# Second batch's Q, K and tail transposes: DMA transposes by halves of the heads in place of identity matmuls

## The chip, the cores and the metric

One core of one Trainium2 chip. The metric is device microseconds (us) of one execution, taken as the median of several. Most executions of one kernel agree within 0.3%; a run over 1.5% above the fastest of the same kernel is called slow, and only fast runs are compared. Positions are times from the start of the profiled execution's span, which is about 1.5 to 2 us shorter than the time of the run.

## The reference, cut to what matters

Cosine attention on 8 batches of 12 heads of 448 x 64, then a Fourier mix, a layer norm and a two-layer feed-forward (FFN):

```python
q_n = q / (norm(q) + 1e-6); k_n = k / (norm(k) + 1e-6)
attn = softmax(q_n @ k_n.T / tau)            # 448 x 448 per head
x    = (attn @ v) as (batch, 448, 768)
u    = x + real(fft(fft(x, axis=1), axis=2))
out  = u + relu(layernorm(u) @ w_ch1) @ w_ch2   # 768 -> 3072 -> 768
```

## The kernel before

Attention of batch b+1 runs beside the FFN of batch b, so that TensorE always has FFN matmuls to put between the attention's. A program-wide list scheduler fixes each engine's order when the kernel is built. Every change of a dependency can therefore reorder instructions far from it.

A batch's 12 heads are handled as six pairs. In the first two batches Q and K come in by halves of three pairs. Of the 448 rows, 384 are "main" and 64 are "tails". For each half: squares on ScalarE (ACT), sums and reciprocal norms, then scaling on VectorE (DVE) into bf16 buffers, then a transpose, because the scores need the head's 64 features on partitions.

The buffers that scaling writes in the second batch:

```python
qh = [[qf[:, 1152 * g:1152 * g + 1152], qf[:, 2304:3456], qf[:, 3456:3840]] for g in range(2)]   # K, Q, tails
```

The transposes, by multiplying with an identity, one pair at a time (j = 0, 1, 2), each with its eviction from PSUM:

```python
for j in range(3):
    def fn(pe, ...):                                    # K of pair j
        for t in range(3):
            r = pe.matmul(PS[.., 128*t:128*t+128], kh[:, 384*j+128*t : ..+128], ID, start=True, stop=True)
    P.add("pe", fn, ...);  evac(tile, self.KT[:, jj, :], 384, ...)
    def fn(pe, ...):                                    # Q of pair j: rows interleaved by 3, tail, column 448
        o3 = o[:, 0:384].rearrange("p (k t) -> p t k", t=3)
        for t in range(3): pe.matmul(o3[:, t], q3[:, t], ID, start=True, stop=True)
        pe.matmul(o[:, 384:448], th[..], ID[:, 0:64], ...);  pe.matmul(o[:, 448:449], q3[:, 0], ID[:, 0:1], ...)
    P.add("pe", fn, ...);  evac(tile, self.QT[:, jj, 0:449], 449, ...)
self.tails(...)                                          # K tails: 3 matmuls, two copies
```

So QT of a pair is 449 columns in order. The scores read it forward and backward (NK = 225 columns each, SQ2 = 450 together):

```python
for c0, cols in ((0, slice(0, NK)), (NK, slice(S, NK - 2, -1))):
    for h in (0, 1):
        pe.matmul(PS[:, bk + h, c0:c0 + NK], KT[r, jj, kt*128:(kt+1)*128], QT[r, jj, cols], start=True, stop=True)
```

The second FFN matrix (W2) is loaded during this same stretch, in twelve chunks of 384 KB issued by GpSimd (POOL). The second batch's raw Q and K wait in memory that later holds W2, so chunks 5 to 11 are held until the scalings have read them:

```python
for c in range(5, 12):
    self.w[12 + c].deps.update(self.raw1[2] + (self.raw1[3] if c > 7 else []))
```

SyncE (SP) issues the third batch's loads of Q and K, and is also the engine that issues DMA transposes.

## Time and profile before

| | before |
|---|---|
| time, median (range) of 4 runs | 617.77 us (617.31 to 618.76) |
| span of the profiled execution, mean clock | 616.0 us, 0.994 |
| TensorE (PE) busy | 591.1 us |
| first exponential of the second batch | 76.40 us |
| last exponential of the second batch ends | 101.77 us |
| first matmul of the second batch's FFN | 129.63 us |
| from there to the end of the span | 486.4 us |

The prediction shows the busy table, the stretches and the chain of waits. The stretch table for the start of the second batch's FFN (span; busy us and count of PE, PEld, DVE, ACT, POOL; clock; DMA share; GB/s):

```profile
136.00:160.00 24.00, 24.00 (x245) 18.60 (x244) 18.64 (x46) 18.56 (x46) 0.00 (x0) 1.00 0.90 161
```

From the timeline of ACT, the end of the first half's exponentials and the beginning and end of the second half's (start, us, what):

```profile
87.17 0.55 ACT L733 ACTIVATE E<-PS 128x450 bf16<-128x450 f32 x1
...
90.91 3.33 ACT L733 ACTIVATE E<-PS 128x900 bf16<-128x900 f32 x4
...
98.72 3.05 ACT L733 ACTIVATE E<-PS 128x900 bf16<-128x900 f32 x4
```

Between the two halves ACT does 3.19 us of other work (87.72 to 90.91).

### The profile page before, as it was taken

The numbers are of one execution on the slowest core, as the hardware profiler recorded it, in microseconds if no ns is written. First come the engines' busy times: TensorE is split into PE (matmuls) and PEld (weight loads), VectorE is DVE, ScalarE is ACT, GpSimd is POOL, SyncE is SP. The second block draws the span as 40 slices with busy tenths as digits, with TensorE's granted clock in tenths as the row PEclk, the third lists the DMA queues.
The fourth block names the chain that finished last, engine by engine and source line by source line (L and its number), as shares of the span: only waits on it lengthen the run. The fifth ranks groups of instructions, "written<-read, shape, count | busy, mean of one in ns | idle before, by whom it ended". The sixth has DMA issues, their size and how long they took to land.

```text
span 616.0 us, 13590 instructions
## 1 busy us (share of the span) xinstructions
PE 591.1 (96%) x5604; PEld 384.7 (62%) x5621; DVE 389.0 (63%) x896; ACT 346.5 (56%) x690; POOL 96.3 (16%) x125
## 2 busy tenths in 40 slices
PE   4788999999999999999999999999999999999998
PEld 3567777667866666655566676566556766654464
DVE  7887987797778677877788669667643670010011
ACT  7784797247873688347745856685576125104300
POOL 8721512010004102010030130003000010010010
PEclk8899999999999999999999999999999999999999
DMA  7999998889339536973196393716720140010001
GB/s 186 120 213 217 159 181 115 95 153 183 76 72 189 122 78 94 131 168 78 30 142 132 95 173 67 162 53 104 58 40 2 53 102 1 27 39 13 1 27 77
DMA packets 187629, 62.02 MB, mean 101 GB/s; under 512 B 166704, under 2 KB 185264, under 8 KB 187568
## 3 DMA queue, kind: packets, MB, share of 16 engines
q1 hardware_dynamic: 129648, 38.35, 32.4%
q0 software_dynamic: 57920, 22.81, 28.8%
q8 instruction: 44, 0.72, 0.5%
q14 instruction: 17, 0.14, 0.1%
HBM read 51.90 MB, written 11.01 MB: 102 GB/s over the span
## 4 chain that ended last, share of the span: by engine, by line
PE 87%; DVE 6%; ACT 2%; POOL 2%; issue 2%; DMA 1%; POOLq 0%; DVEq 0%; ACTq 0%
PE PS L1000 34%; PE PS L1022 34%; PE PS L782 5%; PE PS L751 5%; PE PS L779 2%; PE PS L847 2%; PE PS L882 2%; ACT E L733 2%; DVE U L903 1%; DMA VB<-in_v_dram 1%; DVE ST L930 1%; PE PS L763 1%; PE PS L764 1%; PE PS L1097 1%; DVE OUTB L1031 0%
## 5 line engine op out<-in xcount | busy, mean ns | idle before, releaser
L1000 PE MATMUL PS<-UNT,W1b 128*128 128x256 bf16 (+3 forms) x1424 | 230.6, 315 | 3.4 <-issue 1.3
L1022 PE MATMUL PS<-W2b,hT 128*128 128x384 bf16 (+2 forms) x1343 | 229.7, 326 | 0.1
L1000 PEld LDWEIGHTS PS<-UNT,W1b 128*128 128x128 bf16 x1440 | 129.2, 98 | 87.2 <-ACT hT L1009 3.0
L1022 PEld LDWEIGHTS PS<-W2b,hT 128*128 128x128 bf16 x1344 | 128.8, 98 | 81.9 <-issue 2.6
L733 ACT ACTIVATE E<-PS 128x900 bf16<-128x900 f32 (+1 forms) x192 | 150.0, 826 | 42.6 <-PE PS L751 35.1
L1009 ACT ACTIVATE hT<-PS 128x384 bf16<-128x384 f32 (+3 forms) x170 | 81.0, 477 | 94.7 <-PE PS L1000 93.2
L1031 DVE TENSOR_TENSOR OUTB<-PS,U 128x384 f32<-128x384 f32 (+2 forms) x56 | 31.2, 557 | 116.1 <-PE PS L1022 115.2
L1052 POOL DMA_INDIRECT out_dram<-OUTB,IDX x20 | 22.0, 1099 | 328.2 <-DVE OUTB L1031 188.8
L668 DVE TENSOR_REDUCE SS<-QH 128x6 f32<-128x384 f32 x84 | 45.4, 541 | 14.0 <-ACT QH L666 13.8
L1010 DVE TENSOR_SCALAR hT<-PS 128x256 bf16<-128x256 f32 (+3 forms) x70 | 35.3, 505 | 27.6 <-PE PS L1000 26.4
L782 PE MATMUL PS<-VB,E 128*128 128x65 bf16 x1152 | 51.2, 193 | 0.0
L782 PEld LDWEIGHTS PS<-VB,E 128*128 128x128 bf16 x1152 | 47.7, 97 | 1.7
L666 ACT ACTIVATE QH<-STG 128x384 f32<-128x384 f32 x84 | 43.6, 519 | 7.2 <-DVE SS L668 4.3
L713 POOL DMA_DIRECT2D VB<-in_v_dram x24 | 25.3, 1063 | 128.7 <-PE PS L782 127.8
L751 PE MATMUL PS<-QT,KT 64*128 64x225 bf16 x576 | 43.1, 262 | 2.0 <-ACT E L733 1.7
L779 PE MATMUL PS<-VZ,E 128*128 128x130 bf16 x192 | 42.3, 220 | 1.5 <-DMA VB<-in_v_dram 1.2
L903 DVE TENSOR_TENSOR U<-SQT,X 128x384 bf16<-128x384 f32 (+3 forms) x80 | 40.8, 551 | 0.8
L675 DVE TENSOR_TENSOR QH<-STG,RN 128x768 bf16<-128x768 f32 x42 | 39.7, 950 | 0.5
L796 DVE TENSOR_TENSOR X<-PS,RD 128x512 bf16<-128x512 f32 x48 | 33.2, 691 | 1.5
L751 PEld LDWEIGHTS PS<-QT,KT 64*128 64x128 bf16 x576 | 21.3, 94 | 20.0 <-ACT E L733 8.7
L794 DVE RECIPROCAL RD<-PS 128x8 f32<-128x8 f32 x48 | 9.9, 206 | 32.2 <-PE PS L782 32.0
L857 ACT ACTIVATE Tt<-PS 128x900 bf16<-128x900 f32 (+2 forms) x15 | 13.4, 893 | 28.1 <-PE PS L847 28.1
(117 smaller groups left out, 485.4 us busy)
## 6 DMA issues: line engine op xcount, KB each, us to landing
STG<-in_q_dram SPq DMA_DIRECT2D x18, 384.0 KB, 5.0
STG<-in_k_dram SPq DMA_DIRECT2D x18, 384.0 KB, 4.0
VB<-in_v_dram POOLq DMA_DIRECT2D x24, 192.0 KB, 6.3
W1b<-in_moe_w_ch_dram POOLq DMA_DIRECT2D x12, 384.0 KB, 8.2
W2b<-in_moe_w_ch_dram POOLq DMA_DIRECT2D x12, 384.0 KB, 6.2
out_dram<-OUTB SPq DMA_DIRECT2D x7, 384.0 KB, 2.4
hT<-in_k_dram SPq DMA_DIRECT2D x2, 576.0 KB, 5.4
hT<-in_q_dram SPq DMA_DIRECT2D x2, 576.0 KB, 6.9
```

The source lines that it names most:

```text
L666: P.add("act", lambda a, sq=sq, src=buf[:, w * x:w * x + w]: a.activation(sq, src, ACTF.Square), t_act(w), pr, f"sq{i}_{b}", reads=bn, wri ...
L668: P.add("dve", lambda v, o=SS[:, i, H // ns * x:H // ns * (x + 1)], sq=sq: v.tensor_reduce(o, sq.rearrange("p (h d) -> p h d", d=DH), AX.X ...
L675: P.add("dve", lambda v, i=i, buf=buf, qh=qh: v.tensor_tensor(v3(qh), v3(buf), RN[:, i, :].unsqueeze(2).to_broadcast((128, H, DH)), AluOp. ...
L733: return a.activation(o, self.PS[:, bk:bk + nc_, 0:SQ2], ACTF.Exp, scale=1.0 / self.tau)
L751: i = pe.matmul(self.PS[:, bk + h, c0:c0 + NK], self.KT[r, jj, kt * 128:(kt + 1) * 128], self.QT[r, jj, cols], start=True, stop=True)
L779: pe.matmul(o, st(6), self.VZ[:, j, :], start=True, stop=False, skip_group_check=True)
L782: r = pe.matmul(o[:, 65 * h:65 * h + 65], st(2 * kt + h), self.VB[:, kt, 2 * j + h, :], start=False, stop=(h == 1 and kt == 2), skip_group ...
L903: return v.tensor_tensor(U[o0:o0 + n, ut, cs].rearrange("p (i e) -> p i e", e=2), src, X[i0:i0 + n, x, cs].rearrange("p (i e) -> p i e", e ...
L1000: r = pe.matmul(self.PS[:, bk, 0:n], self.W1b[:, j, ft * 128:(ft + 1) * 128], unT[:, j, cs], start=(j == 0), stop=(j == NJ - 1))
L1009: return e.activation(self.hT[:, ft, cs], self.PS[:, bk, 0:n], ACTF.Relu)
L1010: return e.tensor_relu(self.hT[:, ft, cs], self.PS[:, bk, 0:n])
L1022: r = pe.matmul(self.PS[:, bk, 0:n], self.hT[:, ft, 128 * i:128 * i + 128], self.W2b[:, ft, c0:c0 + n], start=(ft == 0), stop=(ft == NF - 1))
```

## The change

Its intent is to take 54 transposing matmuls off TensorE, and their PSUM evictions off ACT and DVE, by letting the DMA transpose K, and Q with the tails, of one half in one transfer each. The change's DMA transposes don't interleave the rows by three as the matmul's output pattern did, so Q lies in three blocks of 128 columns, and the scores read it as three interleaved thirds (a step of 128 bf16 elements between neighbours, 256 bytes), in three pieces instead of two: 225 forward, 65 of the tail, 162 backward.

```diff
+            if b == 1:
+                qt = flat(self.QT[:])[:, 1536 * g:1536 * g + 1536]
+                for nm, o, i, n, src, wr in (("K", flat(KT of the half), qh[g][0], 9, ...),
+                                             ("Q", qt, qf[:, 2304:3840], 12, ...)):
+                    self.P.add("sp", ... sy.dma_start_transpose(o, i).then_inc(sem, 16) ...)
+                ...  two tail copies (QT -> KTD), one duplicated column on POOL
+                continue
...
+            def qcols(r, jj):
+                if b != 1:
+                    return [(0, self.QT[r, jj, 0:NK]), (NK, self.QT[r, jj, S:NK - 2:-1])]
+                a, x = self.QT[r, 3 * (jj // 3), 0:1], 384 * (jj % 3)
+                return [(0, gp(a, [[1, NK // 3], [128, 3]], x)), (NK, gp(a, [[-1, 65]], 1152 + 128 * (jj % 3) + 64)),
+                        (NK + 65, gp(a, [[-1, 54], [-128, 3]], x + 383))]
...
-                        for c0, cols in ((0, slice(0, NK)), (NK, slice(S, NK - 2, -1))):
+                        for (c0, q0), (_, q1) in zip(*[qcols(r, jj) for r in rs]):
```

More of the change, by code (lines that the diff above doesn't have):

```diff
@@ L585, in first_norm @@
             self.raw1.append(sc)
+            if b == 1:
+                qt = flat(self.QT[:])[:, 1536 * g:1536 * g + 1536]
+                for nm, o, i, n, src, wr in (
+                        ("K", flat(self.KT[:, 3 * g:3 * g + 3, :]), qh[g][0], 9, qhn[g][0], [f"KT{t}" for t in range(3)]),
+                        ("Q", qt, qf[:, 2304:3840], 12, qhn[g][1] + qhn[g][2], [f"QT{t}" for t in range(4)] + ["QTd"])):
+                    o = o.rearrange("p (t c) -> p t c", c=128)
+                    self.P.add("sp", lambda sy, sem, o=o, i=i: sy.dma_start_transpose(o, i).then_inc(sem, 16), 1.45, pg[g], f"tr{nm}{g}_{b}",
+                               reads=src + [x + y for x in src for y in ("_1", "_2")], writes=[f"{x}_{3 * g + y}" for x in wr for y in range(3)],
+                               dma=(f"t{nm}{g}", 16), serve=0.3 * n)
+                tl = qt[:, 1152:1536].rearrange("p (j c) -> p j c", j=3)
+                for x in range(2):
+                    rows = slice(64 * x, 64 * x + 64)
+                    self.copy(self.KTD[rows, 3 * g:3 * g + 3, 64 * x:64 * x + 64], tl[rows, :, 64:128], 192, 4, pg[g], f"ktd{b}",
+                              reads=[f"QTd_{3 * g + y}" for y in range(3)], writes=[f"KTD{x}_{3 * g + y}" for y in range(3)])
+                self.P.add("pool", lambda p, qt=qt, tl=tl: p.tensor_copy(tl[:, :, 64:65], qt[:, 0:1152].rearrange("p (j c) -> p j c", j=3)[:, :, 0:1]), 0.2, pg[g],
+                           f"qdup{b}", reads=[f"QT0_{3 * g + y}" for y in range(3)], writes=[f"QTd_{3 * g + y}" for y in range(3)])
+                continue
             def evac(tile, dst, n, nm, wr):
@@ L747, in fn @@
                         bk, jj = self.bank(tile), ORDER[ps]
-                        for c0, cols in ((0, slice(0, NK)), (NK, slice(S, NK - 2, -1))):
-                            for h in (0, 1):
-                                r = slice(64 * h, 64 * h + 64)
-                                i = pe.matmul(self.PS[:, bk + h, c0:c0 + NK], self.KT[r, jj, kt * 128:(kt + 1) * 128],
-                                              self.QT[r, jj, cols], start=True, stop=True)
+                        rs = [slice(64 * h, 64 * h + 64) for h in (0, 1)]
+                        for (c0, q0), (_, q1) in zip(*[qcols(r, jj) for r in rs]):
+                            for h, mv in ((0, q0), (1, q1)):
+                                n = math.prod(mv.shape[1:])
+                                i = pe.matmul(self.PS[:, bk + h, c0:c0 + n], self.KT[rs[h], jj, kt * 128:(kt + 1) * 128], mv,
+                                              start=True, stop=True)
                     return i
@@ L762, in fn @@
                 bk = self.bank(tile)
-                pe.matmul(self.PS[:, bk, 0:NK], self.KTD[:, j, :], self.QT[:, j, 0:NK], start=True, stop=True)
-                return pe.matmul(self.PS[:, bk, NK:SQ2], self.KTD[:, j, :], self.QT[:, j, S:NK - 2:-1],
-                                 start=True, stop=True)
+                for c0, mv in qcols(slice(0, 128), j):
+                    n = math.prod(mv.shape[1:])
+                    r = pe.matmul(self.PS[:, bk, c0:c0 + n], self.KTD[:, j, :], mv, start=True, stop=True)
+                return r
             self.last_qk = P.add("pe", fn, 0.2, pj, f"qk{j}t_{b}", reads=qreads(j) + [f"KTD0_{j}", f"KTD1_{j}"], tiles=(tile,), acquire=tile,
```

## The prediction

> **What bounds the kernel now.** I read first the page's busy table and its 40 slices, then a table by stretches, then the chain of waits, then the order of instructions around the second batch's attention.
>
> ```profile
> PE 591.1 (96%) x5604; PEld 384.7 (62%) x5621; DVE 389.0 (63%) x896; ACT 346.5 (56%) x690; POOL 96.3 (16%) x125
> ...
> PE   4788999999999999999999999999999999999998
> DVE  7887987797778677877788669667643670010011
> ACT  7784797247873688347745856685576125104300
> ```
>
> TensorE is nearly full except in the first four slices (62 us); VectorE is high there and low at the end. The change acts once, in the second batch, so what matters is whether that batch's attention gates anything. The stretches (span, then busy us and count of PE, PEld, DVE, ACT, POOL, then clock, DMA share, GB/s):
>
> ```profile
> 68.00:92.00 24.00, 22.13 (x279) 16.73 (x278) 20.88 (x50) 20.67 (x40) 4.75 (x7) 1.00 1.13 171
> 92.00:130.00 38.00, 38.00 (x350) 26.43 (x348) 31.02 (x77) 18.18 (x39) 6.33 (x7) 1.00 0.78 111
> 130.00:136.00 6.00, 5.65 (x51) 4.21 (x49) 5.13 (x13) 3.28 (x10) 1.64 (x2) 1.00 0.91 192
> 136.00:200.00 64.00, 64.00 (x660) 46.82 (x658) 50.12 (x120) 41.76 (x92) 6.23 (x7) 1.00 0.82 129
> ```
>
> From 68 to 92 us, where Q, K and tails are transposed, TensorE idles only 24.00 - 22.13 = 1.87 us, but DVE and ACT are 86 to 87% busy. From 92 us on TensorE has no idle but 0.35 us at 130. So everything after 130 us is fixed TensorE work, and the end moves with the start of the second FFN. What sets that start, from the chain of waits (start, us, what):
>
> ```profile
> 113.22 4.89 PE PS L1022 x30
> 118.13 0.56 DVE OUTB L1031
> ...
> 123.44 0.21 DVE MV L932
> ...
> 128.93 0.06 DVE F L939
> 128.98 0.34 issue
> 129.32 0.95 DVE QH L675
> 130.27 0.48 DVE OUTB L1031
> 130.80 5.30 PE PS L1000 x45
> ```
>
> From 118 us the chain leaves TensorE and runs through VectorE: the second batch's residual, layer norm and their evictions. The timeline puts the second FFN's first matmul at 129.63 us. The two normalised tiles that it needs are ready at 126.29 us; with 2.8 us to land a transpose that is about 129.1. So TensorE runs out of first-FFN work within about half a microsecond of the second batch's tiles arriving. **Two paths are level here**: TensorE's own work, and the second batch's attention through ACT and DVE. The change shortens the first and touches the second.
>
> The order around the first half of the heads (start, us, engine, line, operation):
>
> ```profile
> 73.89 0.28 DVE L571 TENSOR_TENSOR QH<-W2b,RN 128x128 bf16<-128x128 f32 x1
> ...
> 75.36 0.56 PE L751 MATMUL PS<-QT,KT 64*128 64x225 bf16 x8
> ...
> 76.40 0.92 ACT L733 ACTIVATE E<-PS 128x900 bf16<-128x900 f32 x1
> ```
>
> Scaling of this half ends at 74.17, but by then its first pair of heads is already transposed: scores at 75.36, first exponential at 76.40. The last exponential of the batch ends at 101.77. That is 25.4 us for 24 exponentials costing 19.0 us of ACT.
>
> **What the Trainium skill says.** "DMA: Bandwidth & Descriptors", section Issuing engines are not separate DMA queues: transfers of every issuing engine share the same 16 DMA engines and interleave. The trace agrees that they are shared: a DMA share over 1 and 171 GB/s in this stretch, while weight chunks take 6.2 to 8.2 us to land. The same page, section DMA Transpose (X-bar): it works on 2-byte data and writes SBUF, so no PSUM and no eviction; the later batches use it, rows below. "TensorE: Matmul & The Clock Gate", section Part 4: PE-mode transpose: TensorE's output goes to PSUM and needs a copy after it. This kernel multiplies by an identity as an ordinary matmul, and the trace shows that copy as the evictions below. "Advanced Engine Details and Errata", section SBUF Cachelines: a read that changes the 16-byte line at each access pays a penalty. The new thirds step 128 bf16, 256 bytes. No matmul here has such a moving operand; the existing reversed one costs nothing (261 ns against 262 forward). This is open.
>
> **The change part by part.** The transposes and their evictions, from the groups by shape for 68 to 92 us (busy us, mean ns):
>
> ```profile
> L611 PE MATMUL PS<-ID,QH 128*128 128x128 bf16 x18 | 3.0, 301 | 0.1
> L590 ACT ACTIVATE QT<-PS 128x449 bf16<-128x449 f32 x4 | 2.2, 549 | 0.6 <-PE PS L613 0.3
> L590 DVE CAST KT<-PS 128x384 bf16<-128x384 f32 x4 | 2.1, 549 | 0.0
> ```
>
> *Removed from TensorE*: 54 matmuls. In the timeline a group for Q (three strided, the tail, one column) holds the array about 0.45 us, one for K 0.20, one for tails 0.16: 6 x 0.45 + 6 x 0.20 + 2 x 0.16 = 4.2 us. (Busy figures of these lines overlap their neighbours, so they aren't added.)
>
> *Added to TensorE*: each of 18 score blocks goes from 4 matmuls to 6, each of 6 tail blocks from 2 to 3: 42 more, the columns still 450. The 65-column piece can't start much faster than the warm-up matmuls of 62 columns, one per 30 ns (73 in 2.23 us). Estimate: 40 ns more a block, 24 x 0.04 = 1.0 us. Net -3.2 us if the stride is free.
>
> *Removed from ACT and DVE*: KT and QT evictions, 3.15 us on ACT and 3.37 on DVE. The tail copies stay, from SBUF now (0.3 to 0.5 us each), plus two small copies on GpSimd, 0.3 to 1.0 us each (that line in the later batches has 261 to 998 ns).
>
> *Added to the DMA*: four transposes. The present ones carry 128x768:
>
> ```profile
> QT<-QH SPq DMA_TRANSPOSE x24, 3.1
> KT<-QH SPq DMA_TRANSPOSE x18, 4.5
> ```
>
> The last number is median us from issue to landing; issuing takes 1.2 to 1.3 us, the minimum is 2.7 and the maximum 9.2. A K half is 1.5 times as large, a Q half with tails twice. By issue time alone: K 1.9 us and Q 2.5 us, and 2 us more to land; shared with weight chunks I take 6 to 8 us for Q.
>
> *Moved*: the wait becomes coarse. Q can leave only when all three pairs and tails are scaled, 74.17 less about 0.7 us of evictions no longer between: 73.5. Then 6 to 8 us of transfer, about 1.2 us for tail copy and duplicated column (in series, each with a semaphore), 0.6 us of scores and waits. The first exponential comes at 81.3 to 83.3 instead of 76.40, 5 to 7 us later. But ACT and DVE don't lose that time: they do the second half's squares, sums and scalings in it, now done at 88.44; I expect about 83, so the second half's transposes land near 90, before the first half's exponentials end (10 us after they start), and the present gap between halves, 87.72 to 90.91, closes. From the first exponential on ACT needs the 19 to 20 us of exponentials and about 2.5 us of ReLU evictions and the next batch's squares: end near 81.3 + 22.5 = 103.8 to 105.8, against 101.77. So +2 to +4 us on the attention path; less the half microsecond of slack at 129 us and about 0.7 us of lighter DVE, **+1 to +3 us** at the start of the second FFN. TensorE's 3.2 us don't show: it waits for that start.
>
> **The rivals.** (1) *The saving counts*: if transfers land in 4 us, ACT relief makes up for the late start, attention ends as before or sooner, and up to 3.2 us is gained, 615 us. For it: quiet landings of 2.7 us; against it, 171 GB/s of other traffic and the coarse wait. (2) *The SP queue blocks*: the third batch's loads leave at 83.11 us, when the weight chunk that they wait for lands, and take till 88.78 to issue. If the second half's transposes stand behind them in SP's fixed order, they land 6 to 8 us late and the end is +5 to +7, 624 us. (3) *The stride slows matmuls*: 387 of 450 columns in 24 blocks, 161 ns a block at full rate; at half rate 24 x 0.161 = 3.9 us more, which only cancels TensorE's saving, and shows as 0 to +1 us. (4) *Weight chunks come late*: 1.4 MB more, some 7 us at 200 GB/s, while the last W2 chunk lands near 102 and is used from about 106. Against it: two holes, 74 to 78 us at 103 to 127 GB/s and 82 to 84 at 45, and that the chunks gated on the scalings (three at 74.58, three at 88.86) leave earlier.
>
> **Range and chances.** The middle is 617.75 + 1.5 = 619.2 us: +1 to +3 weighted with rival 1 (about 30%) and rival 2 (about 15%). Range 614.5 to 623.5. Two per cent is 12.4 us: a gain of that size would exceed all that is removed, and a loss needs rivals 2 and 4 together. Faster 0.02, same 0.94, slower 0.04.
>
> **What would show it.** First exponential of the second batch at 81 to 83 us, no gap between its halves, last one at 104 to 106; the second FFN's first matmul 1 to 3 us after 129.63, with 3 to 5 us of TensorE idle before it where there is none now; from there to the end the same 486 us. Q transposes 6 to 8 us to landing. The 225-column score matmul at its 261 ns if the stride is free. I am wrong if the second FFN starts before 129 us, if the matmuls of the thirds are far longer, or if TensorE's idle time comes after 136 us.

## The result, and the profile after

The changed kernel took **637.62 us**, the median of all its runs (fast ones of 635.71, 637.10 and 638.14, a slow one of 648.18), against 617.77 before. Ratios in this document are the mean time of one kernel's fast runs over that of the other's fast runs of the same rounds, so not quite the ratio of the medians quoted. Here it is 1.0309, with a 95% interval of 1.028 to 1.0338: slower. The results are correct. Lines moved down by the change: the exponentials are L752 now (L733 before), the scores L778 and L792, the FFN's first product L1028 and its second L1050, the transposes L594.

The head of the page of the changed kernel (busy us and share, then tenths in 40 slices of 15.9 us):

```profile
span 635.1 us, 13600 instructions
...
PE 598.1 (94%) x5609; PEld 385.9 (61%) x5609; DVE 388.5 (61%) x889; ACT 344.5 (54%) x685; POOL 94.7 (15%) x127
...
PE   4878995987999999999999999999999999999998
...
PEclk9998997997999999999999999999999999999999
```

The span grew by 19.1 us. TensorE's busy time didn't fall but rose by 7 us. About 2 us of this rise are not real: the trace before lacks 17 matmul records (5604 matmuls beside 5621 weight loads), which leaves 2.16 us of holes from 270 to 600 us, where the trace after has none. There are two dents in its row, in the seventh slice (95 to 111 us) and in the ninth and tenth (127 to 159 us). The row of the clock falls in the seventh and the tenth too. The stretches of the changed kernel:

```profile
68.00:92.00 24.00, 22.94 (x229) 16.39 (x229) 15.92 (x40) 16.13 (x35) 6.88 (x11) 1.00 1.40 172
92.00:130.00 38.00, 30.07 (x334) 19.78 (x331) 16.69 (x42) 19.58 (x34) 5.27 (x7) 0.87 0.95 116
130.00:136.00 6.00, 6.00 (x42) 3.73 (x40) 5.63 (x12) 2.23 (x5) 1.12 (x1) 1.00 0.67 145
136.00:160.00 24.00, 17.40 (x131) 12.40 (x130) 18.66 (x45) 10.80 (x35) 1.20 (x2) 0.86 0.68 130
```

From 92 to 130 us TensorE lost 7.93 us and from 136 to 160 us 6.60 us, where before there was no hole in either stretch. DVE did 16.69 us of work from 92 to 130 us where it did 31.02 before: the second batch's work hadn't arrived. What held it is in the chain of waits (start, us, what):

```profile
84.53 1.95 PE PS L1050 x12
87.05 2.55 ACT E L752 x3
89.83 14.44 DMA QT<-QH
104.27 0.74 issue
105.01 0.64 PE PS L778 x6
...
141.53 0.93 DVE ST L958 x2
146.79 21.86 PE PS L1028 x180
```

One transfer, the Q transpose of the second half, carries 14.44 us of the chain. TensorE's own rows in the timeline name the same two waits (the bracket holds the idle time just before, and what ended it):

```profile
105.01 1.07 PE L778 MATMUL PS<-QT,KT 64*128 64x225 bf16 x12 [5.74 <-DMA QT<-QH]
...
146.79 0.80 PE L1028 MATMUL PS<-UNT,W1b 128*128 128x256 bf16 x3 [6.60 <-DVE SS L687]
```

The releaser in the second row is only the one that came last by the profile; the weight load just before that matmul waited for "DMA UNT<-F", the transposes of the normalised tiles, which began at 141.56 us. That is the second batch arriving late at its FFN.

What became of the four transposes. SP's timeline (start, issue time, what; each transfer ends some time after its issue):

```profile
72.20 1.35 SPq L594 DMA_TRANSPOSE KT<-QH  x1
75.14 3.71 SPq L594 DMA_TRANSPOSE QT<-QH  x1
82.42 2.03 SPq L594 DMA_TRANSPOSE KT<-QH  x1
88.41 0.62 SPq L679 DMA_DIRECT2D STG<-in_q_dram  x1
89.08 0.65 SPq L679 DMA_DIRECT2D STG<-in_k_dram  x1
89.83 10.36 SPq L594 DMA_TRANSPOSE QT<-QH  x1
```

From issue to landing these took 7.4, 9.5, 6.9 and 14.4 us. Between the third and the fourth stand two loads of the third batch, and SP's table of waits shows how long they held the queue (us in total, times, longest):

```profile
SPq L679 <- DMA W2b<-in_moe_w_ch_dram: 3.9, 1, 3.9
```

The two loads of 192 KB each landed after 10.1 and 12.1 us, at 98.47 and 101.2. From 89.83 to 98.47 us, the first 8.6 us of Q's flight, SP's queue moved 0.39 MB, which is just what the two loads hold, and in every trace here SP's transfers land in the order of their issue. So Q's transpose stood behind the loads in flight too, and not only for the 2.5 us before its issue.

And the exponentials, from ACT's timeline:

```profile
87.05 3.04 ACT L752 ACTIVATE E<-PS 128x900 bf16<-128x900 f32 x4 [2.10 <-PE PS L778]
...
97.47 0.55 ACT L752 ACTIVATE E<-PS 128x450 bf16<-128x450 f32 x1 [0.57 <-PE PS L792]
104.29 0.36 ACT L1089 ACTIVATE KTD<-QT 64x192 bf16<-64x192 bf16 x1 [6.28 <-DMA QT<-QH]
105.67 3.00 ACT L752 ACTIVATE E<-PS 128x900 bf16<-128x900 f32 x4 [0.61 <-PE PS L778]
...
118.77 0.55 ACT L752 ACTIVATE E<-PS 128x450 bf16<-128x450 f32 x1 [0.18 <-PE PS L792]
```

Together with the rows before, these give the whole account of the second batch's attention:

| stretch | before | changed | difference |
|---|---|---|---|
| first exponential starts | 76.40 | 87.05 | +10.65 |
| from it to the end of the first half's exponentials | 11.32 | 10.97 | -0.35 |
| gap between the halves | 3.19 | 7.65 | +4.46 |
| second half's exponentials | 10.86 | 13.65 | +2.79 |
| last exponential ends | 101.77 | 119.32 | **+17.55** |
| second FFN's first matmul | 129.63 | 146.79 | **+17.16** |
| from there to the end | 486.4 | 488.3 | +1.9 |

While the second half's exponentials run, TensorE feeds them at half clock: the granted clock was 0.50 from 104 to 112 us, and again 0.50 from 144 to 148, late in the holes of 5.74 and 6.60 us and after them. The clock is not the whole of the 2.79 us, as e1 below shows. Its mean was back at 0.91 in 112 to 116 us and at 1.00 from 116 us. The kernel before shows 1.00 in all these stretches.

Groups of score matmuls by shape, 80 to 125 us of the changed kernel (count | busy us, mean ns | idle before). The means hold some at half clock:

```profile
L778 PE MATMUL PS<-QT,KT 64*128 64x225 bf16 x36 | 7.2, 394 | 7.8 <-DMA QT<-QH 5.7 <-ACT E L752 1.9
L778 PE MATMUL PS<-QT,KT 64*128 64x162 bf16 x36 | 6.0, 326 | 0.0
L778 PE MATMUL PS<-QT,KT 64*128 64x65 bf16 x36 | 3.8, 204 | 0.0
```

So there are four suspects: the landing time of the transposes beside other traffic (A), the place of Q's second transpose behind two loads (B), the strided read of Q (C), and the coarse hand-over by halves itself (D).

### The profile page after: what moved, and what is told of

The parts are those of the page before. It is cut to its first block, busy times and chain, and to the rows that moved or that the text cites. A ratio compares the mean times of both kernels' runs of the same rounds, so it can differ in the third digit from the quotient of the medians.

```text
span 635.1 us, 13600 instructions
## 1 busy us (share of the span) xinstructions
PE 598.1 (94%) x5609; PEld 385.9 (61%) x5609; DVE 388.5 (61%) x889; ACT 344.5 (54%) x685; POOL 94.7 (15%) x127
## 4 chain that ended last, share of the span: by engine, by line
PE 87%; DVE 4%; DMA 3%; POOL 2%; issue 2%; ACT 2%; POOLq 0%; DVEq 0%; ACTq 0%
PE PS L1028 35%; PE PS L1050 34%; PE PS L778 5%; PE PS L810 5%; DMA QT<-QH 2%; PE PS L875 2%; PE PS L807 2%; PE PS L910 2%; ACT E L752 2%; PE PS L792 1%; DMA VZ<-in_v_dram 1%; DVE U L931 1%; PE PS L1125 1%; DVE ST L958 1%; POOL VB L732 1%
## 5 line engine op out<-in xcount | busy, mean ns | idle before, releaser
L1028 PE MATMUL PS<-UNT,W1b 128*128 128x256 bf16 (+3 forms) x1440 | 233.0, 317 | 7.9 <-DVE SS L687 6.6
L1050 PE MATMUL PS<-W2b,hT 128*128 128x384 bf16 (+2 forms) x1344 | 230.6, 327 | 0.0
L1028 PEld LDWEIGHTS PS<-UNT,W1b 128*128 128x128 bf16 x1440 | 129.8, 98 | 94.0 <-DMA UNT<-F 7.0
L1050 PEld LDWEIGHTS PS<-W2b,hT 128*128 128x128 bf16 x1344 | 128.7, 98 | 82.9 <-issue 3.8
L752 ACT ACTIVATE E<-PS 128x900 bf16<-128x900 f32 (+1 forms) x192 | 149.7, 824 | 51.4 <-PE PS L778 44.0
L1080 POOL DMA_INDIRECT out_dram<-OUTB,IDX x20 | 20.6, 1031 | 316.8 <-DVE OUTB L1059 251.2
L778 PE MATMUL PS<-QT,KT 64*128 64x225 bf16 (+2 forms) x612 | 46.8, 269 | 10.5 <-DMA QT<-QH 5.7
L778 PEld LDWEIGHTS PS<-QT,KT 64*128 64x128 bf16 x612 | 23.2, 96 | 31.2 <-ACT E L752 11.8
```

What stands on the lines that cost most here:

```text
L752: return a.activation(o, self.PS[:, bk:bk + nc_, 0:SQ2], ACTF.Exp, scale=1.0 / self.tau)
L778: i = pe.matmul(self.PS[:, bk + h, c0:c0 + n], self.KT[rs[h], jj, kt * 128:(kt + 1) * 128], mv, start=True, stop=True)
L1028: r = pe.matmul(self.PS[:, bk, 0:n], self.W1b[:, j, ft * 128:(ft + 1) * 128], unT[:, j, cs], start=(j == 0), stop=(j == NJ - 1))
L1050: r = pe.matmul(self.PS[:, bk, 0:n], self.hT[:, ft, 128 * i:128 * i + 128], self.W2b[:, ft, c0:c0 + n], start=(ft == 0), stop=(ft == NF - 1))
```

## The experiments

Fifteen kernels ran, in four groups; the kernels of a group ran on one chip and share their runs of the kernel before. "WRONG" marks kernels whose scores read Q's columns in an order that is not the right one. The kernel before had medians of 617.13, 616.31, 617.34 and 617.30 us in the four groups. The table has the medians (of all runs, slow ones with them), the ratio of the fast runs with its interval, and four times from the profiles (us).

| kernel | median | ratio to before (95%) | first exp. | last exp. ends | FFN starts | span |
|---|---|---|---|---|---|---|
| before | 617.77 | | 76.40 | 101.77 | 129.63 | 616.0 |
| the change | 637.62 | 1.0309 (1.0280 to 1.0338) | 87.05 | 119.32 | 146.79 | 635.1 |
| e1_contig (WRONG) | 638.71 | 1.0358 (1.0338 to 1.0378) | 87.30 | 117.56 | 144.88 | 633.4 |
| e2_spfirst | 635.94 | 1.0272 (1.0218 to 1.0326) | slow | slow | slow | slow |
| e3_spfirst_wlate | 630.99 | 1.0231 (1.0209 to 1.0254) | 86.48 | 111.33 | 141.35 | 629.2 |
| e4_all_contig (WRONG) | 631.35 | 1.0231 (1.0213 to 1.0248) | 84.64 | 110.18 | 140.78 | 628.3 |
| e5_half0 | 640.73 | 1.0376 (1.0331 to 1.0422) | 91.03 | 123.74 | 150.65 | 638.0 |
| e6_half1 | 629.26 | 1.0203 (1.0186 to 1.0220) | 76.08 | 111.28 | 138.62 | 628.2 |
| e9_pairs | 633.40 | 1.0272 (1.0238 to 1.0306) | 84.63 | 115.71 | 144.10 | 630.6 |
| e10_dummy | 633.74 | 1.0266 (1.0243 to 1.0289) | 75.24 | 112.83 | 141.38 | 633.0 |
| e7_pe_thirds | 621.25 | 1.0073 (1.0053 to 1.0092) | 76.11 | 104.79 | 132.65 | 619.5 |
| e8_k1 | 621.68 | 1.0071 (1.0058 to 1.0084) | 74.56 | 100.75 | 128.12 | 619.3 |
| e11_dummy_free | | two fast, two slow runs | 78.58 | 103.97 | 131.84 | 618.8 |
| e12_quiet | 622.33 | 1.0079 (1.0065 to 1.0094) | 84.40 | 109.14 | 134.25 | 621.3 |
| e13_quiet_contig (WRONG) | 619.34 | 1.0038 (1.0019 to 1.0056) | 82.36 | 104.07 | 130.47 | 617.4 |
| e14_w8late | 633.90 | 1.0266 (1.0245 to 1.0287) | slow | slow | slow | slow |
| e15_k_quiet | 621.56 | 1.0059 (1.0044 to 1.0074) | 81.31 | 106.95 | 132.99 | 619.9 |

### First group: the strided read, the place in the queue, the traffic

**e1_contig** changes only the order in which the two large pieces of Q are read, to whole runs of neighbours instead of a step of 256 bytes. The count of columns, and every engine's order, is the same.

```diff
-                return [(0, gp(a, [[1, NK // 3], [128, 3]], x)), ...
-                        (NK + 65, gp(a, [[-1, 54], [-128, 3]], x + 383))]
+                return [(0, gp(a, [[128, 3], [1, NK // 3]], x)), ...
+                        (NK + 65, gp(a, [[-128, 3], [-1, 54]], x + 383))]
```

> The changed kernel with the same instructions in the same order on every engine; only the two access patterns of the thirds are turned from interleaved to block order, so that each matmul reads runs of contiguous columns (the scores come out in another order: wrong result on purpose). If the stride is a main cause, the 225-column score matmul falls from 394 ns to about 262, six matmuls of a block from 0.59 us to about 0.4, and the time by 3 to 6 us (24 blocks x 0.2 us on the chain of scores and exponentials, less what hides). If the wait for the transposes decides alone, the time stays within 1.5 us of the changed kernel's 637.

It took 638.71 us: no gain. The matmuls did become shorter (225 columns: 300 ns in the mean instead of 394, 162 columns: 264 instead of 326, half-clocked ones in all four), but the last Q transpose landed after 15.5 us, and the first exponentials of both halves came when they had come before (87.30, and 105.68 against 105.67). In its profile, which is of its fastest run, the second half's exponentials took 11.88 us, where the change has 13.65 and the kernel before 10.86: at half clock the stride made up 1.8 of the 2.8 us. But the runs as a whole show nothing of it. With the transfers setting the time, suspect C is not the cause of the loss.

**e2_spfirst** only puts SP's loads of the third batch behind the last transpose:

```diff
-   ... dma=(key, 16 * len(dm)), after=gate, serve=1.75))
+   ... dma=(key, 16 * len(dm)), after=gate, serve=1.75, order=self.tr1[3:] if b == 2 else []))
```

> The changed kernel with one change of order on SP: the second half's Q transpose is queued ahead of the third batch's first two loads (in the changed kernel it was issued at 89.83 us behind them although its data was ready at 87.3). If the place in SP's queue is the main cause, that transpose lands some 8 us sooner and the time falls by 6 to 9 us. If the sharing with the weight chunks is the main cause, it is issued 2.5 us sooner but still takes about 10 us or more to land, and the time falls by 2 to 5 us.

Its fast runs were 630.0, 634.57 and 637.32 us, its interval overlaps that of the change, and the profile fell in a slow run. Inconclusive as to what the queue alone costs; mending it leaves the kernel slower by over 2% in any case.

**e3_spfirst_wlate** does that and holds the weight chunks: chunks 5 to 7 until the first half's Q has landed, 8 to 11 until the second half's has.

```diff
-   self.w[12 + c].deps.update(self.raw1[2] + (self.raw1[3] if c > 7 else []))
+   self.w[12 + c].deps.update(self.raw1[2] + (self.raw1[3] if c > 7 else []) + [self.tr1[1 if c < 8 else 3]])
```

> As the run before, and the W2 chunks 5 to 7 wait for the first half's Q transpose to land, chunks 8 to 11 for the second half's. If sharing with weight chunks is what makes the transposes slow, the first half's Q lands in 5 to 6 us instead of 9.5, the second half's likewise instead of 14.4, first exponential near 83 instead of 87, and the time falls by 8 to 13 us against the changed kernel (unless the late W2 chunks stall the first FFN's second product, which would show as waits of L1050 for W2 transfers). If a transpose of this size is slow by itself, landing stays at 8 us and more and the time is as in the run before.

630.99 us: a quarter (by the ratios) to a third (by the medians) of the loss came back. Landings were 7.4, 5.6, 9.2 and 8.7 us; chunks 5 to 7 still ran beside the second half's transposes. The last exponential ended at 111.33 us, 8 us sooner than in the change. The expectation for the first half failed: its Q landed at 80.9 us, 3.8 us sooner, but the first exponential came at 86.48 instead of near 83, because TensorE, in its new fixed order, ran FFN matmuls until the first scores at 85.85.

**e4_all_contig** is e3 with e1's reads.

> The run before plus contiguous reads (wrong result on purpose). If the three causes (queue place, sharing, stride) make up the loss, the time is 3 to 5 us below the run before, at about 618 to 624; if it stays above 626 a fourth cause is left.

631.35 us, the same ratio as e3. The stride still doesn't count where transfers decide.

### Second group: one half alone, finer pieces, and transposes that nobody uses

**e5_half0** and **e6_half1** make the change in the first or the second half of the heads only (e6 also with the loads behind its transposes):

```diff
-            if b == 1:
+            if b == 1 and g == 0:          # e5;  g == 1 in e6
...
-                if b != 1:
+                if b != 1 or jj // 3 != 0: # e5;  != 1 in e6
```

> Only the first half of the heads goes by DMA with thirds; the second half is transposed by TensorE as before. Theory of the late start (the second FFN inherits what the batch's exponentials end later): first exponential near 86 us as in the changed kernel, no second wait, exponentials end near 108 instead of 101.77, time 622 to 627. If the loss sits in the second half's transposes (place in the queue, chunks of weights), this run is within 2 us of before.

640.73 us, worse than both halves together. The half's Q transpose took 15.1 us to land, and the first exponential came at 91.03 us, so the expected 622 to 627 us were far off. The weight chunks issued beside it were slow as well, 14.6 to 15.7 us. From 80 to 88 us the transpose and the chunks together moved only 99 GB/s at a DMA share of 1.28; in the change, from 89.83 to 98.47 us, plain loads and chunks together moved 197 GB/s.

> Only the second half goes by DMA, its Q transpose queued ahead of the third batch's loads; the first half as before. Late start: first exponential at 76.4 as before, second half's first exponential near 98 instead of 90.9, since its Q is scaled by 87 to 88 and takes 7 to 10 us to land; time 622 to 626. If the first half alone makes the loss: 617 to 619.

629.26 us. Here the first half runs as before, and the transpose, first in its queue, lands 7.3 us after its issue at 89.26 us. The exponentials of the second half in ACT's timeline of e6:

```profile
88.27 0.56 ACT L752 ACTIVATE E<-PS 128x450 bf16<-128x450 f32 x1
96.57 0.36 ACT L1089 ACTIVATE KTD<-QT 64x192 bf16<-64x192 bf16 x1 [2.48 <-DMA QT<-QH]
98.46 2.98 ACT L752 ACTIVATE E<-PS 128x900 bf16<-128x900 f32 x4 [1.52 <-PE PS L778]
```

The gap between the halves is 9.63 us (88.83 to 98.46), against 3.19 before. So a single transfer of 7.3 us, with no queue before it but beside three weight chunks, put the second half 7.5 us later (98.46 against 90.91) and the FFN's start 9.0 us later. The two half-changes don't add up to the whole (+24 and +13 us against +20): the loss is not a sum of costs per transfer but of what each wait meets.

**e9_pairs** hands over pair by pair instead of by halves: 18 smaller transposes, loads behind them, chunks held as in e3.

```diff
+                for j in range(3):
+                    for nm, o, i, n, rd, wr in (("K", KT of pair, qh[g][0][:, c3], 3, ...), ("Q", qt[:, c3], lh[:, c3], 3, ...),
+                                                ("T", tail of pair, th[:, 128 * j:128 * j + 128], 1, ...)):
+                        ... sy.dma_start_transpose(o, i) ...
```

> All by DMA, but pair by pair: for each of the six pairs of heads its own transposes of K (three tiles), Q (three) and tails (one), issued as soon as that pair is scaled; W2 chunks and the third batch's loads wait as in the run with the order mended and the late chunks (631.0). If the coarse wait for a whole half is what costs, the first exponential comes near 81 instead of 86.5 and the time falls to 622 to 627. If the latency of any transpose through the busy DMA engines is what costs, the first exponential stays at 85 or later and the time at 629 to 633.

633.40 us, no better than e3. With a third or a quarter of the data, the pieces of K and the first one of Q in each half still took 7.7 to 9.0 us to land; later pieces took 2.4 to 6.9. The first exponential came 1.9 us sooner than in e3, the second FFN 2.7 us later. So the smaller grain bought nothing in this form, and suspect D, in the sense of "too coarse", finds no support: what a first piece costs here is hardly its size.

**e10_dummy** is the kernel before with the same four transposes added, into spare memory that nobody reads. TensorE still transposes; only the traffic, the queue place and the reading of the scaled buffers are added.

```diff
+            if b == 1:
+                for nm, o, i, n, src in (("K", self.UNT[:, 2304:3456], qh[g][0], 9, ...), ("Q", self.UNT[:, 3456:4992], qf[:, 2304:3840], 12, ...)):
+                    P.add("sp", ... sy.dma_start_transpose(o, i) ..., reads=src + ..., writes=["SCR" + nm] + ...)
```

> The kernel before with its TensorE transposes, and beside them the changed kernel's four DMA transposes of the same data into a spare buffer that no score reads. If the waits for the transposes make the loss, time is 617 to 620. If their load on the DMA engines does (weight chunks and the third batch's loads late), it is 623 or more.

633.74 us: a loss nearly as large as the change's, with the identity matmuls still in place. Its timeline shows a wait that I had not thought of (DVE's scaling of the second half, then TensorE's transposes):

```profile
94.88 0.56 DVE L576 TENSOR_TENSOR QH<-W2b,RN 128x384 bf16<-128x384 f32 x1 [10.20 <-DMA UNT<-QH]
...
95.70 0.82 PE L616 MATMUL PS<-ID,QH 128*128 128x128 bf16 x3 [9.35 <-DVE QH L572]
```

The scaling of the second half's Q waited for the dummy transpose of the first half to land, because both halves share the buffer. The dummy of that Q took 21.7 us to land, far longer than any transpose in the change, so e10's loss can't be carried over in size. In the changed kernel the second half's Q is scaled from 85.20 us on, also only after the first half's transpose had landed at about 84.7, but DVE stood still for just 1.92 us before it. An identity matmul frees that buffer as soon as it has run; the transpose by DMA held it for its whole flight.

### Third group: the stride by itself, K alone, free traffic, quiet

**e7_pe_thirds** is the kernel before (TensorE transposes) with Q laid out in thirds and read as in the change.

```diff
-                    o3 = o[:, 0:384].rearrange("p (k t) -> p t k", t=3)
+                    o3 = o[:, 0:384].rearrange("p (t k) -> p t k", t=3) if b == 1 else ...
...
+            def qcols(r, jj): ...                       # as in the change
```

> The scores' part of the change alone: TensorE still transposes, but writes the second batch's Q in the changed kernel's layout, and the scores read it in interleaved thirds with 42 more matmuls. The stride was seen to lengthen a 225-column matmul from 262 to 394 ns, 24 blocks x 0.2 us = 5 us more TensorE and score time. If that goes to the end: 621 to 623. If it hides behind the exponentials: 616 to 619.

621.25 us, +3.9 us by the medians, with TensorE's busy time at 595.97 instead of 591.08 us. Where no transfer decides, the strided reads, the 42 more matmuls and Q's evictions, which this layout needs in two pieces each, cost about four microseconds together.

**e8_k1** moves only K of the second half to the DMA, in the kernel before; K is read without a stride.

```diff
+            if b == 1 and g == 1:
+                P.add("sp", ... sy.dma_start_transpose(o, i) ...)       # K of the half
-                P.add("pe", fn, 0.3, ..., f"tk{jj}_{b}", ...);  evac(tile, self.KT[:, jj, :], 384, ...)
+                if not (b == 1 and g == 1): (the same two)
```

> The kernel before with one of the four DMA transposes: K of the second half alone, whose data is scaled at 80.2 us and first read at 90.4, 10 us later, so that a landing in 4 to 9 us is hidden. Nine matmuls and three evictions go. If the loss comes from waits, the time is 615.5 to 617.5, perhaps a little under before. If any such transpose in this stretch disturbs the weight chunks and loads: 620 or more.

621.68 us; I had not expected a loss. The transfer was issued at 78.48 us and landed in 6.5 us, long before it was needed; the attention ended 1.0 us sooner and the FFN started 1.5 us sooner than before. Yet from there to the end it took 491.2 us instead of 486.4. TensorE idles 2.7 us near 128 us, and from 200 to 300 us it was busy for 96.50 us instead of 98.85, with a granted clock of 0.82 from 212 to 216 us and 0.88 from 216 to 224 where the kernel before has 1.00. The order fixed at the build differs from that of the kernel before all over this part; why it is worse is not settled. It warns that differences of 4 us between kernels with different orders can be the order's alone.

**e11_dummy_free** is e10 with the dummies reading weights instead, so that nobody waits for them:

```diff
+                for nm, o, i, n in (("K", self.UNT[:, 2304:3456], self.W1b[:, 0, 0:1152], 9), ("Q", self.UNT[:, 3456:4992], self.W1b[:, 1, 0:1536], 12)):
+                    ... reads=[f"W1_{x}" for x in range(6)], after=[...] + (sc[0::3] if nm == "K" else sc), ...
```

> As the run with the dummy transposes (633.7), where the second half's scaling of Q turned out to wait 9.3 us for the first half's dummy transpose, because both halves share one buffer; here the dummies read weights instead, so that nothing in the attention waits for them. If waits are the whole loss: 616 to 619. If the load on the DMA engines costs by itself (weight chunks, loads of the third batch, V): 622 or more.

Two runs of 619.11 and 620.57 us, and two of 630.78 and 633.31 that count as slow. If the fast ones stand, traffic alone cost 2 to 3 us and the waits for the buffer and the queue the rest of e10's 17 us.

**e12_quiet** is the change with the loads behind the transposes and all chunks from 5 on held until the last transpose has landed.

```diff
-   self.w[12 + c].deps.update(self.raw1[2] + (self.raw1[3] if c > 7 else []))
+   self.w[12 + c].deps.update(self.raw1[2] + (self.raw1[3] if c > 7 else []) + [self.tr1[3]])
```

> The changed kernel with the second half's Q transpose ahead of the loads, and all W2 chunks from 5 on held back until that transpose has landed, so that no weight chunk runs beside the three later transposes. If sharing with weight chunks is what makes them slow, they land in 4 to 6 us each, and the second half's first exponential follows the first half's last without a gap. The time may still be 625 to 635, since the W2 chunks come late; the verdict is in the landings. If they still take 8 us and more, the size of the transposes is the cause.

622.33 us, correct, and the ratio is 1.0079: of the 20 us lost, 15.3 by the medians (14 by the ratios) came back. From SP's and POOL's timelines of e12:

```profile
71.05 1.43 SPq L594 DMA_TRANSPOSE KT<-QH  x1
73.87 5.66 SPq L594 DMA_TRANSPOSE QT<-QH  x1
81.27 1.29 SPq L594 DMA_TRANSPOSE KT<-QH  x1
85.49 1.61 SPq L594 DMA_TRANSPOSE QT<-QH  x1
89.79 2.14 POOL L471 DMA_DIRECT2D W2b<-in_moe_w_ch_dram  x3 [6.79 <-DMA QT<-QH]
```

The first two, still beside earlier chunks and loads of V, landed after 9.8 and 8.4 us; the last two, with neither a weight chunk nor a load in flight, after 3.2 and 3.7. The quiet is thus both: e12 moves the third batch's loads away as well as the chunks. The stretch table of e12 shows the quiet:

```profile
72.00:76.00 4.00, 4.00 (x39) 3.12 (x37) 3.10 (x7) 2.44 (x8) 0.00 (x0) 1.00 1.60 185
...
83.00:86.00 3.00, 3.00 (x28) 1.96 (x29) 2.81 (x8) 1.99 (x3) 0.00 (x0) 1.00 0.36 67
```

The DMA share is 1.60 where the first two were in flight and 0.36 at the second half's turn. The second half's Q landed at 89.2 us, before the first half's exponentials ended at 95.74, and TensorE had no long hole any more. Same transposes, same stride, same halves, and three quarters of the loss gone: as far as the new order that comes with new waits lets one say it, suspects A and B together carry the loss.

### Fourth group: what is left

**e13_quiet_contig** is e12 with e1's reads, with the same order on all engines as e12.

> The run with all later W2 chunks held back (622.3), same instructions in the same order, with contiguous reads in place of the thirds (wrong result on purpose). If the stride is what is left of the loss, TensorE's busy time falls by about 5 us and the time to 616.5 to 619. If the time stays within 1 us of 622.3, what is left is the late start of the attention.

619.34 us, 3.0 us less than e12 (1.0038 against 1.0079, intervals apart). The score matmuls of e12, 70 to 125 us by shape:

```profile
L778 PE MATMUL PS<-QT,KT 64*128 64x225 bf16 x36 | 7.1, 393 | 2.2 <-ACT E L752 2.1
L778 PE MATMUL PS<-QT,KT 64*128 64x162 bf16 x36 | 5.8, 317 | 0.0
```

And of e13:

```profile
L778 PE MATMUL PS<-QT,KT 64*128 64x225 bf16 x36 | 4.7, 267 | 3.3 <-ACT E L752 3.2
L778 PE MATMUL PS<-QT,KT 64*128 64x162 bf16 x36 | 4.1, 228 | 0.0
```

At full clock the step of 256 bytes makes a 225-column matmul 126 ns longer, 0.56 ns a column. TensorE's busy time fell from 592.72 to 589.84 us, and the time by 3.0 us. (The trace of e12 lacks 17 matmul records, which leaves 1.70 us of holes from 270 to 600 us, and that of e13 lacks none; with them the busy time fell by 4.6 us.) The stride is a real cost, but one that shows only when transfers no longer decide.

**e14_w8late** is the change in its own order, with only chunks 8 to 11 held:

```diff
-   (self.raw1[3] if c > 7 else [])
+   (self.raw1[3] + [self.tr1[3]] if c > 7 else [])
```

> The changed kernel with SP's order as it was (the second half's Q behind the first two loads of the third batch), and only the W2 chunks 8 to 11 held until that transpose has landed. If the chunks beside it made its 14.4 us, it lands in 6 to 8 us and the second half starts near 98 instead of 105.7: time 626 to 632. If its place behind the loads did, it still lands after 12 us or more and the time stays at 634 to 638.

Fast runs of 633.07 to 635.51 us, 1.0266: some 3 us better than the change by the ratios, with intervals that just overlap. The profile fell in a slow run. Holding these four chunks is far from enough; what e12 gains comes from the rest as well, the chunks 5 to 7, the loads and the new order.

**e15_k_quiet** tries for a version that beats both kernels: K of both halves by DMA, Q by TensorE with no stride, chunks held until the second K has landed.

```diff
+            if b == 1:
+                self.trk = P.add("sp", ... sy.dma_start_transpose(o, i) ...)   # K of each half, as in e8_k1
...
+   ... + [self.trk]                                                            # chunks 5 to 11
```

> What the experiments point to: K of both halves by DMA, Q and tails by TensorE (so no stride), W2 chunks from 5 on held until the second K has landed. 18 matmuls and six evictions go. If waits and stride are the loss, 614.5 to 617.5, at or a little under before; if the first K lands late (its scores wait at 75 us, it is ready at 71), 618 to 621.

621.56 us, correct, and no gain where I had expected one. The first exponential comes at 81.31 us, 4.9 us later than before, and the second FFN starts 3.4 us later. No version that I tried beats the kernel before.

## Why the prediction was right or wrong

**Wrong in the result.** It gave 619.2 us with a range up to 623.5 and a chance of 0.04 for slower by over 2%; the time was 637.62 us.

**The frame held**: "everything after 130 us is fixed TensorE work, and the end moves with the start of the second FFN." From that start to the end it was 486.4 us before, 488.3 in the change, and 486.5 to 488.5 in all other kernels with a fast profile but e6 (489.6), e8 (491.2) and e10 (491.6). The start moved by 17.16 us and the span by 19.1. Also as predicted, TensorE idled just before it (6.60 us; 3 to 5 expected), and the saved transposes were worth nothing, since TensorE waited. Two of the three signs of being wrong that it named came true: the idle time lay after 136 us (140.19 to 146.79), and the matmuls of the thirds took 393 ns for 261.

**The step that failed is the landing of the transposes**, "6 to 8 us for Q" and "the second half's transposes land near 90": Q took 9.5 us and then 14.4, and the second landed at 104.2. By the prediction's own terms:

| term | predicted | changed kernel |
|---|---|---|
| first half's Q can leave | 73.5 | 75.14 (scaling ends at 75.07) |
| Q to landing, first half | 6 to 8 | 9.5 |
| tail copy and duplicated column, to the scores | 1.2 | 1.77 |
| scores to first exponential | 0.6 | 0.64 |
| first exponential | 81.3 to 83.3 | 87.05 |
| second half scaled | about 83 | 87.30 |
| its Q issued | at once | 89.83, 2.5 us later |
| Q to landing, second half | some 7 | 14.4 |
| second half's Q landed | near 90 | 104.2 |
| gap between halves | closes | 7.65, from 3.19 |

For the second half the 14.2 us are 4.3 of later scaling, 2.5 of queue before the issue and 7.4 of longer flight, in which the queue has a part again. The first half's scaling ended 1.6 us later than I took it to be: it began 0.93 us later than in the kernel before (69.41 against 68.48), and it took 5.66 us where it had taken 5.69, so the 0.7 us of evictions no longer between didn't show.

*Later scaling*: the prediction let DVE scale the second half while the first half's Q was in flight. It could not, as Q of both halves has one buffer; e10 showed that wait by itself (10.20 us). The line of code that shows it stood in the kernel, and I had not read it for this. In the change DVE's wait for that landing and the tail copies behind it made 2.4 of the 4.3 us. The norms were ready only at 82.77 us and the scalings take 2.1 us, so without the wait they would have ended near 84.9; my 83 was 1.9 us too early.

*Queue*: this is rival 2, given 15%, 6 to 8 us of late landing and +5 to +7 us at the end. It happened to Q. The issue was 2.5 us late, because the loads before it waited for a weight chunk that had taken 10.4 us (7.1 before), and in flight it stood behind these loads again. Beside weight chunks a Q half landed after 7.3, 8.7 and 10.3 us where it stood before the loads (e6, e3, e4), and after 14.4 and 15.5 behind them (the change, e1). No run shows its share of the end alone, since e2 was inconclusive.

*Flight*: I scaled the issue times of the later batches' transposes (medians of 3.1 and 4.5 us to landing) by size, and added a share for the weight chunks. The size was not the error: without that share my sum gives 4.5 us for a Q half (2.5 + 2), and in quiet it landed after 3.6 and 3.7 (e13, e12). In company it took up to 15.5 us (e1), and a dummy that no score waits for 21.7 (e10). In the trace a transpose is made of 256-byte packets (1536 for a Q half) and a weight chunk of 1536-byte ones. Small packets alone can't be the whole cause: the plain loads have packets of 256 bytes too, and with the chunks they moved 197 GB/s in the change, where transposes and chunks moved 99 in e5 (80 to 88 us), 157 in e4 and 185 in e3 (84 to 94 us both). Why the engines moved less when a transpose took part, and by such different amounts, no run isolates. Rival 4 asked whether the chunks would come late, not what the chunks do to the transposes. The three chunks gated on the first scaling did come late (8.8 to 10.4 us to landing, 4.8 to 7.1 before); TensorE didn't wait for them, but the loads that held up Q did.

**What was not in the sum at all:** after a hole of 5.74 us TensorE ran at half clock for about 8 us, with the second half's exponentials 2.8 us longer (1.0 us with contiguous reads, e1), and the FFN began at half clock, which fits the +1.9 us after its start. I had foreseen 3 to 5 us of idle time without asking for the clock.

**The prediction comes close to e13 instead**, a kernel that is wrong and holds the chunks. With the chunks held, the order mended and no stride, the first half's Q landed in 6.2 us (6 to 8), the first exponential came at 82.36 (81 to 83), the last ended at 104.07 (103.8 to 105.8), and the FFN started 0.84 us later (just under +1 to +3). Its 619.34 us are close to the predicted 619.2, partly by luck: the second half's Q landed at 87.3 (near 90), and the gap between the halves fell to 1.6 us and didn't close. The chain from landing to exponentials to FFN was right; the contention, the queue in flight and the shared buffer were missing.

**The stride** (rival 3: 3.9 us at half rate, to show as 0 to +1 us) had about the right size: 3.0 us in e13 against e12, and 3.9 with TensorE's transposes (e7), where the added matmuls and evictions are in it. In the change itself it showed as nothing (e1), as rival 3 said, though because the transfers decided. TensorE's net saving without the stride looks smaller than my 3.2 us, 591.08 to 589.84 us of busy time; with the 2.16 us that the missing records take from the trace before it is 3.4 us, as predicted.

**The account of the loss**, by the medians: 637.62 us to 622.33 by quiet and queue order (-15.3, e12), to 619.34 by contiguous reads (-3.0, e13), and 2 us to the kernel before (617.30 in those rounds). These last 2 us are unsettled: 0.84 of them are the later start, and e8, which loses 4 us though its FFN starts sooner than before, shows that a new fixed order can cost as much. (e15's 4 us are mostly its later start, 3.4 us.) Nor can e12 be split between quiet, queue and the new order that comes with them; only e1 against the change and e13 against e12 are pairs with one order.

## What to carry to other kernels

Cost a transpose that moves to the DMA by its landing beside the traffic of just that moment, and not by the median of the others; then ask what its flight holds up: the buffer that it reads, the queue that it stands in, what stands before it there, and what stands behind it. Work taken from an engine that waits for another path was worth nothing here, and the holes of about 6 us on TensorE cost more than their length, because the granted clock fell to 0.50 with them. When a loss is found, remove the traffic first: a suspect such as a strided read can look free as long as something slower decides.

## What the Trainium skill lacked or had wrong

- "Advanced Engine Details and Errata", section X-Bar Transpose (TRN2): "TRN2 transpose DMAs are as fast as regular DMAs". The runs agree in quiet: a Q half, as large as a load (384 KB), landed in 3.6 to 3.7 us with nothing beside it (e13, e12). Beside weight chunks it is less sure: transposes and chunks together moved 99 GB/s (e5, 80 to 88 us), 157 (e4, 84 to 94) and 185 (e3, 84 to 94), plain loads of the same packet size and chunks 197 (the change, 89.83 to 98.47). One landing time by itself misleads: the 14.4 us of the change were spent partly behind two plain loads that took 10.1 and 12.1 us, with half the data each.
- "DMA: Bandwidth & Descriptors", section Issuing engines are not separate DMA queues, says that transfers interleave, but gives no figure for what this costs: from 89.83 to 98.47 us of the change the weight chunks moved 1.30 MB and everything that SP had issued 0.39 MB.
- "Advanced Engine Details and Errata", section SBUF Cachelines, names a penalty without a size. Measured on TensorE: a moving operand with a step of 256 bytes took 393 ns for 225 columns against 267 for contiguous runs, 0.56 ns more a column; a contiguous but reversed one cost nothing in the kernel before (261 ns against 262).
- No page has what it costs that a DMA transpose holds its source until it lands: a second scaling into the same buffer waited 10.20 us in e10, where an identity matmul frees the buffer once it has run.
